# Where the projection of four short chunks falls among the steps, one product's place beside a burst, and three more idle matmuls in the head

## The chip, the core and the metric

The kernel runs on one core of a Trainium2 chip. TensorE (PE in the profile) multiplies matrices, ScalarE (ACT) and VectorE (DVE) work elementwise, GpSimd (POOL) and SyncE (SP) mostly issue DMAs here. The metric is the time of one execution on the device in microseconds (us). Unprofiled, the kernel before takes 773.35 us, the median of three runs (773.33 to 774.28).

## The reference

The input x is 8 sequences of 3008 tokens with 256 channels. Each channel is filtered along the sequence (a real Fourier transform, a product with a complex filter, the transform back), and each of the 24064 tokens then goes through two matrices with a "snake" activation between them:

```python
X = np.fft.rfft(x, axis=1)                       # 8 x 3008 x 256
y = np.fft.irfft(X * (filt_r + 1j * filt_i)[None], n=3008, axis=1)
h = y.reshape(24064, 256) @ w_in                 # 256 -> 2048
s = np.sin(alpha * h)
out = (h + s * s / (alpha + 1e-09)) @ w_out      # 2048 -> 256
```

Inputs and output are float32; the kernel works in float16 with float32 sums.

## The kernel before

**The two halves of the work.** The Fourier filter is a two-stage transform written as matmuls with tables. For a sequence b the parts are: `load_x` (a DMA), `first` or `first_tiled` (matmuls into PSUM tiles `pa`), a turn through DRAM (`load_t2`), `forward` (matmuls into `pb`, a copy to `xf` on ScalarE, and a DMA that swaps the halves of `xf` into `xs`), `product` (VectorE, L257: `xf` times the filter's real part), `cross` (VectorE, L263 and L264: `xs` times the imaginary part, and the sum), `inverse` or `inverse_tiled` (matmuls into `pc`), again a turn through DRAM (`load_t4`), and `last` (matmuls into `pd`, copied into `y`). Sequence 0 is done in the head of the program, before the steady loop, with its own functions.

The second half works on chunks of tokens: 48 chunks, twelve for each pair of sequences, 512 tokens each except the sixth of each pair, which has 384 (chunks 5, 17, 29 and 41; L597). `hidden(k, jb)` (L603) makes one of sixteen tiles of chunk k: two matmuls of 512 (or 384) columns into a PSUM tile `ph`, a sine on ScalarE (`cos_all`, L614), and one operation on VectorE (`v`, L615, called STT below) that also sets the PSUM tile free. `project(k, u)` (L619) is half of a 128-token block of the second product: eight matmuls of 256 columns into `po`. After an odd u of the second block, and of the last block, ScalarE copies the result (L639) and a DMA stores it.

**The order.** All engines execute in the order in which the program is written, and this order comes from the loop at L759. Chunk k has eight steps. A step writes two `hidden` tiles of chunk k, then what is due of the Fourier work (`slot(step)`), then the share of `project` for chunk k-1, then `slot(step + 0.5)`. A chunk of 512 tokens has eight halves to project, one in each step. One of 384 has six for eight steps, so two steps stay without.

The Fourier work lies in the list `pending` with due times in steps, set by formulas at L709 to L742. At certain times, the list `bursts` (L693), four or eight matmul groups come at once: `first_tiled` or `inverse_tiled`. A burst takes two PSUM tiles from the pool `fps` and two from the pool `hps`; each is copied out by ScalarE (two or three of them) and VectorE (two or one). `aside` (L699) moves a `product` or a `cross` that falls shortly before a burst to just behind it.

**PSUM.** The `ph` tiles and the burst's second pair share the four buffers of `hps` in turn: a tile can be begun when the tile four places earlier has been read for the last time, by STT or by the burst's copy. The two buffers of `fps` hold `pa`, `pb`, `pd` and the burst's first pair; the two of `ops` hold `po`.

**The head.** Before the loop, TensorE transforms sequence 0. `spread_alpha` (L349) brings alpha to all partitions with twelve small matmuls into a tile of `hps`. `inverse_table` (L426) turns a table with sixteen transposes into a tile `pse` of `ops`, from which ScalarE makes the table `t_a`. `warm_pe(n)` (L438) issues n matmuls of 512 columns on a zero tile, into a tile of `hps` that nobody reads.

Of the kernel before, what the change touches and what calls it, by code (L numbers as in the profile page):

```python
# [71 lines left out]
def kernel(  # L72
# [276 lines left out]
    def spread_alpha(i):  # L349

        ps = hps.tile([128, 4, 128], FP32, name=f"al_bc_{i}", tag="h")
        for a in range(4):
            for k, part in enumerate(parts):
                nc.tensor.matmul(out=ps[:, a, :], lhsT=one[:, 4 * i + a:4 * i + a + 1].to_broadcast([128, 128]),
                                 rhs=part, start=(k == 0), stop=(k == 2))
        nc.scalar.copy(out=alpha[:, i // 2, 512 * (i % 2):512 * (i % 2) + 512], in_=ps.rearrange("p a b -> p (a b)"))
# [69 lines left out]
    def inverse_table(g):  # L426

        gs = slice(8 * g, 8 * g + 8)
        ps = ops.tile([128, 8, 128], FP16, name=f"pse_{g}", tag="o")
        for i in range(8):  # L430
            for a in range(2):
                nc.tensor.transpose(out=ps[64 * a:64 * a + 64, i, :],
                                    in_=d_t[:, 8 * g + i, 64 - 64 * a:128 - 64 * a], identity=id16)
        nc.scalar.mul(e1_0[:, gs, :], ps, -0.125)
# [3 lines left out]
    def warm_pe(n):  # L438

        warmed.append(n)  # L440
        ps = hps.tile([128, 512], FP32, name=f"warm_{len(warmed)}", tag="h")
        for i in range(n):
            nc.tensor.matmul(out=ps, lhsT=idle[:, 0:128], rhs=idle[:, 0:512], start=True, stop=True)
# [18 lines left out]
    for i in range(16):  # L462
# [7 lines left out]
        if i < 15 and i % 4 == 3:  # L470
            warm_pe((1, 2, 2, 1)[i // 4])
    spread_alpha(0)
    [inverse_table(g) for g in range(2)]
    spread_alpha(1)
    warm_pe((2, 2, 2, 1)[3])
# [127 lines left out]
    def hidden(k, jb):  # L603

        _, c0, n = chunks[k]
        if jb == 0:
            v[k] = vpool.tile([128, 16, 512], FP16, name=f"v_{k}", tag="v")
        ps = hps.tile([128, 512], FP32, name=f"ph_{k}_{jb}", tag="h")
        for cb in range(2):
            nc.tensor.matmul(out=ps[:, 0:n], lhsT=w1[:, cb, jb * 128:jb * 128 + 128],  # L610
                             rhs=y_cols[:, cb, c0:c0 + n], start=(cb == 0), stop=(cb == 1))
            one_between()
        cs = cos_all[:, jb % 4, :]
        nc.scalar.activation(out=cs[:, 0:n], in_=ps[:, 0:n], func=AFT.Sin, bias=float(np.pi / 2))  # L614
        marks["snake"] = nc.vector.scalar_tensor_tensor(  # L615
            out=v[k][:, jb, 0:n], in0=cs[:, 0:n], scalar=-1.0, in1=ps[:, 0:n],
            op0=ALU.add, op1=ALU.subtract)

    def project(k, u):  # L619

        pb, c0, n = chunks[k]
        t, half = divmod(u, 2)
        rest = len(chunks) - 1 - k
        alone = rest == 0 or rest == 1 and t > 1
        if rest == 0 and t > 1:
            t = 5 - t
        if (t % 2 == 0 or alone) and half == 0:
            pso[k] = ops.tile([128, 2, C], FP32, name=f"po_{k}_{t}", tag="o")
        for jb in range(8 * half, 8 * half + 8):
            nc.tensor.matmul(out=pso[k][:, t % 2, :], lhsT=v[k][:, jb, 128 * t:128 * t + 128],  # L630
                             rhs=w2[:, jb, :], start=(jb == 0), stop=(jb == 15))
            if jb % 2:
                one_between()
        last = 128 * (t + 1) == n
        if half == 1 and (t % 2 == 1 or last or alone):
            i0 = t % 2 if alone else 0
            o = opool.tile([128, 2, C], FP32, name=f"o_{k}_{t}", tag="o")
            copy = nc.vector.tensor_copy if rest == 0 else nc.scalar.copy
            copy(out=o[:, i0:t % 2 + 1, :], in_=pso[k][:, i0:t % 2 + 1, :])  # L639
            for i in range(i0, t % 2 + 1):  # L640
                store(o[:, i, :], pb, c0 + 128 * (t - t % 2 + i),
                      (nc.scalar, nc.sync, nc.scalar, nc.scalar) if rest == 0 and t == 3 else
                      (nc.sync, nc.scalar) if rest == 0 or (rest == 1 and t > 2) else
                      (nc.sync,) if rest < 7 else (nc.gpsimd,))
# [39 lines left out]
    def firsts(b):  # L684

        return {2: (37.5, 39.5, 41.5, 43.5), 3: (49.5, 54.5, 60.5, 66.5)}.get(
            b, [48 * b - 105.5 + 8 * ch for ch in range(4)])

    def inverses(b):

        return (63.5, 73.5, 81.5) if b == 2 else [48 * b - 46.5 + 16 * w for w in range(3)]

    bursts = [at for b in range(TILED, B) for at in (*firsts(b), *inverses(b))]  # L693
# [4 lines left out]

    def aside(at):  # L699

        return next((s + 0.05 for s in bursts if s - 1.1 < at <= s), at)

    for at, fn in put_later:
        put(at, fn)
# [6 lines left out]
    for b in range(1, B):  # L711
        s = s1 if b == 1 else Spectral(b)
# [12 lines left out]
        for u in range(12):  # L725
            inv = 24 + 1.21 * u if b == 1 else 57 + 2.2 * u if b == 2 else z - 59 + 4 * u
            fwd = inv - 6
            fwd = clear(fwd)
            put(fwd, s.forward, u, pe=True)
            put(aside(fwd + (0.5 if b == 1 else 1.5)), s.product, u)  # L730
            if s.fused:
                put(aside(fwd + (4 if b == 1 else 4.5)), s.cross, u)
            if b < TILED:
                put(inv, s.inverse, u, pe=True)
# [10 lines left out]
    def slot(at):  # L745

        run = 0
        while pending and pending[0][0] <= at:
            if pending[0][2]:
                if run and pending[0][0] > at - 1:  # L750
                    break
                run += 1
            _, _, _, fn, args = pending.pop(0)
            fn(*args)
# [4 lines left out]
    for k in range(len(chunks) + 1):  # L759
        for j in range(8):  # L760
            if k < len(chunks) and step > 0:
                hidden(k, 2 * j)
                hidden(k, 2 * j + 1)
            slot(step)
            if k > 0:
                n_half = 2 * (chunks[k - 1][2] // 128)
                for u in range(n_half * j // 8, n_half * (j + 1) // 8):
                    project(k - 1, u)
            slot(step + 0.5)
            step += 1  # L770
# [31 lines left out]
```

## Time and profile before

| What | Value |
|---|---|
| Median of three runs | 773.35 us (773.33 to 774.28) |
| The profiled execution: its own time | 774.35 us |
| its span, from first to last instruction | 772.6 us |
| TensorE clock granted | full (1.000) |
| PE busy | 763.0 us, 99% of the span |
| DVE busy | 655.4 us, 85% |
| ACT busy | 610.9 us, 79% |
| POOL busy | 373.1 us, 48% |
| STT (L615), 512 columns | 704 of 682 ns, 449.9 us |
| Sine (L614), 512 columns | 704 of 609 ns, 385.8 us |
| `project` matmuls (L630) | 3008, a group of eight takes 0.87 us |

"Busy" is time with at least one instruction under way. Neighbouring instructions overlap in their rows: a group of eight `project` matmuls is listed as 1.04 us long, yet the next group starts 0.87 us after it. Two STTs in a row start 0.60 us apart, two sines 0.48 to 0.49 us, two burst copies on ScalarE 0.48 us. In what follows durations that add up are such distances from start to start. In a row of the timeline the first number is the start and the second the length; a bracket at the end tells how long the engine was idle before it, and what ended that.

### The profile page before, as it was taken

The numbers are of one execution on the slowest core, as the hardware profiler recorded it, in microseconds if no ns is written. First come the engines' busy times: TensorE is split into PE (matmuls) and PEld (weight loads), VectorE is DVE, ScalarE is ACT, GpSimd is POOL, SyncE is SP. The second block draws the span as 40 slices with busy tenths as digits, with TensorE's granted clock in tenths as the row PEclk, the third lists the DMA queues.
The fourth block names the chain that finished last, engine by engine and source line by source line (L and its number), as shares of the span: only waits on it lengthen the run. The fifth ranks groups of instructions, "written<-read, shape, count | busy, mean of one in ns | idle before, by whom it ended". The sixth has DMA issues, their size and how long they took to land.

```text
span 772.6 us, 17227 instructions
## 1 busy us (share of the span) xinstructions
PE 763.0 (99%) x6038; PEld 517.1 (67%) x6038; DVE 655.4 (85%) x1171; ACT 610.9 (79%) x1205; POOL 373.1 (48%) x652
## 2 busy tenths in 40 slices
PE   8999999999999999999999999999999999999997
PEld 4757766666666667666666676766666766766666
DVE  7887998999988888988889888899888888777774
ACT  6898987898787878877878787888778787777763
POOL 7555455644636456545555646644554645520000
PEclk9999999999999999999999999999999999999999
DMA  9945678854854437544574536754254322511112
GB/s 225 292 108 167 139 172 257 205 131 112 219 145 125 114 92 207 140 114 118 118 197 114 137 94 156 196 144 121 72 145 109 90 69 56 147 35 33 40 36 61
DMA packets 81598, 101.49 MB, mean 131 GB/s; under 512 B 18900, under 2 KB 60880, under 8 KB 81511
## 3 DMA queue, kind: packets, MB, share of 16 engines
q0 software_dynamic: 27520, 47.29, 26.0%
q1 hardware_dynamic: 53426, 52.41, 25.5%
q8 instruction: 47, 0.77, 0.4%
q10 hardware_dynamic: 565, 0.70, 0.3%
q14 instruction: 40, 0.33, 0.1%
HBM read 56.15 MB, written 46.66 MB: 133 GB/s over the span
## 4 chain that ended last, share of the span: by engine, by line
PE 89%; DVE 5%; DMA 2%; ACT 2%; POOL 1%; issue 1%; SPq 0%; POOLq 0%; DVEq 0%
PE po L630 40%; PE ph L610 40%; DVE v L615 3%; PE pd L316 2%; PE pb L243 2%; PE pa L222 2%; DMA xs<-xf 1%; PE pc L293 1%; DMA e_t<-e_tbl 1%; ACT cos_all L614 1%; DVE t_a L479 1%; ACT t_h L185 1%; PE pa L206 0%; PE pd L409 0%; POOL filt_t L365 0%
## 5 line engine op out<-in xcount | busy, mean ns | idle before, releaser
L615 DVE SCALAR_TENSOR_TENSOR v<-cos_all,ph 128x512 f16<-128x512 f32 (+1 forms) x768 | 482.5, 671 | 94.8 <-ACT cos_all L614 90.8
L614 ACT ACTIVATE cos_all<-ph 128x512 f32<-128x512 f32 (+1 forms) x768 | 414.1, 600 | 99.4 <-PE ph L610 98.8
L675 POOL DMA_DIRECT2D out_dram<-o x530 | 291.7, 557 | 246.0 <-ACT o L639 219.5
L610 PE MATMUL ph<-y,w 128*128 128x512 f16 (+1 forms) x1536 | 389.3, 375 | 1.6 <-DVE v L615 1.3
L630 PE MATMUL po<-w,v 128*128 128x256 f16 x3008 | 389.5, 273 | 0.0
L630 PEld LDWEIGHTS <-v 128*128 128x128 f16 x3008 | 290.0, 98 | 84.2 <-issue 0.9
L610 PEld LDWEIGHTS <-w 128*128 128x128 f16 x1536 | 143.3, 98 | 114.1 <-issue 19.3
L639 ACT COPY o<-po 128x512 f32<-128x512 f32 (+1 forms) x95 | 56.0, 590 | 7.7 <-PE po L630 6.8
L185 ACT CAST y<-pd 128x376 f16<-128x376 f32 (+1 forms) x86 | 42.0, 490 | 13.1 <-PE pd L316 8.8
L246 ACT CAST xf<-pb 128x512 f16<-128x512 f32 x84 | 51.0, 608 | 0.9 <-PE pb L243 0.2
L160 POOL DMA_DIRECT2D x<-in_x_dram x48 | 25.6, 538 | 39.0 <-DVE v L615 29.9
L185 ACT CAST t_h<-pa 128x512 f16<-128x512 f32 (+1 forms) x60 | 32.8, 589 | 12.6 <-PE pa L222 11.3
L316 PEld LDWEIGHTS <-t_a 96*128 96x128 f16 x448 | 31.4, 97 | 12.7
L264 DVE TENSOR_TENSOR p<-p,xs 128x512 f16<-128x512 f16 x84 | 35.7, 425 | 2.9
L263 DVE TENSOR_TENSOR xs<-xs,filt_t 128x512 f16<-128x512 f16 x84 | 35.1, 418 | 3.5 <-DMA xs<-xf 3.5
L257 DVE TENSOR_TENSOR p<-xf,filt_t 128x512 f16<-128x512 f16 x84 | 35.0, 418 | 0.0
L185 ACT CAST gt<-pc 128x512 f16<-128x512 f32 x54 | 28.1, 595 | 8.4 <-PE pc L293 8.4
L187 DVE CAST t_h<-pa 128x512 f16<-128x512 f32 (+1 forms) x52 | 33.5, 682 | 0.2
L243 PE MATMUL pb<-t,d_t 128*128 128x256 f16 x168 | 32.1, 273 | 0.0
L316 PE MATMUL pd<-wh_t,t_a 96*128 96x94 f16 x384 | 31.8, 204 | 0.0
L235 POOL DMA_DIRECT2D t<-d x28 | 24.4, 874 | 10.7 <-DMA d<-t_h 10.0
L243 PEld LDWEIGHTS <-d_t 128*128 128x128 f16 x168 | 16.4, 98 | 14.3
(72 smaller groups left out, 276.5 us busy)
## 6 DMA issues: line engine op xcount, KB each, us to landing
t<-d POOLq DMA_DIRECT2D x28, 384.0 KB, 5.0
xs<-xf SPq DMA_DIRECT2D x168, 64.0 KB
t_a<-d SPq DMA_DIRECT2D x28, 384.0 KB
x<-in_x_dram POOLq DMA_DIRECT2D x50, 188.0 KB, 4.4
d<-t_h SPq DMA_DIRECT2D x48, 192.0 KB
d<-gt SPq DMA_DIRECT2D x36, 256.0 KB
out_dram<-o POOLq DMA_DIRECT2D x91, 64.0 KB, 2.1
out_dram<-o POOLq DMA_DIRECT2D x31, 80.0 KB, 3.3
```

The source lines that it names most:

```text
L185: marks["act"] = nc.scalar.copy(out=dst, in_=src)
L243: nc.tensor.matmul(out=ps[:, i, :], lhsT=d_t[:, s, :], rhs=self.t2[s // 6][:, s % 6, :], start=True, stop=True)
L246: nc.scalar.copy(out=self.xf[u], in_=ps)
L263: nc.vector.tensor_tensor(out=xs, in0=xs, in1=f_t[1][:, 2 * u:2 * u + 2, :], op=ALU.mult)
L264: nc.vector.tensor_tensor(out=p, in0=p, in1=xs, op=ALU.add)
L316: nc.tensor.matmul(out=psv[:, i, :], rhs=wi_t if self.b < TILED else wh_t, start=True, stop=True, lhsT=t4_h[ch // 2][0:NK, n0 % 16 + i, cb ...
L610: nc.tensor.matmul(out=ps[:, 0:n], lhsT=w1[:, cb, jb * 128:jb * 128 + 128], rhs=y_cols[:, cb, c0:c0 + n], start=(cb == 0), stop=(cb == 1))
L614: nc.scalar.activation(out=cs[:, 0:n], in_=ps[:, 0:n], func=AFT.Sin, bias=float(np.pi / 2))
L615: marks["snake"] = nc.vector.scalar_tensor_tensor(out=v[k][:, jb, 0:n], in0=cs[:, 0:n], scalar=-1.0, in1=ps[:, 0:n], op0=ALU.add, op1=ALU. ...
L630: nc.tensor.matmul(out=pso[k][:, t % 2, :], lhsT=v[k][:, jb, 128 * t:128 * t + 128], rhs=w2[:, jb, :], start=(jb == 0), stop=(jb == 15))
L639: copy(out=o[:, i0:t % 2 + 1, :], in_=pso[k][:, i0:t % 2 + 1, :])
L675: queues[i % len(queues)].dma_start(out=bass.AP(tensor=out.tensor, offset=out.offset + t0 * C, ap=[*ap, [1, C]]), in_=o_blk[p0:p0 + rows, :])
```

## The change

Three edits. The halves of a 384-token chunk are dealt to the eight steps by rounding the bounds up, not down: before, steps 0 to 7 of the following chunk get 0, 1, 1, 1, 0, 1, 1, 1 halves, after it 1, 1, 1, 0, 1, 1, 1, 0. Chunks of 512 tokens keep one half in each step. This acts at the chunks that follow chunks 5, 17, 29 and 41, which are steps 48 to 55, 144 to 151, 240 to 247 and 336 to 343. The window of `aside` goes from 1.1 to 1.3 steps. Going through all due times, one item changes: `product` 9 of sequence 2, due at 72.3, goes to 73.55, behind the `inverse_tiled` at 73.5. And `warm_pe(3)` stands in the head between `spread_alpha(0)` and the first two calls of `inverse_table`.

```diff
     spread_alpha(0)
+    warm_pe(3)
     [inverse_table(g) for g in range(2)]
     spread_alpha(1)
...
     def aside(at):
-        return next((s + 0.05 for s in bursts if s - 1.1 < at <= s), at)
+        return next((s + 0.05 for s in bursts if s - 1.3 < at <= s), at)
...
             slot(step)
             if k > 0:
                 n_half = 2 * (chunks[k - 1][2] // 128)
-                for u in range(n_half * j // 8, n_half * (j + 1) // 8):
+                for u in range(-(-n_half * j // 8), -(-n_half * (j + 1) // 8)):
                     project(k - 1, u)
             slot(step + 0.5)
```

## The prediction

> **What bounds the kernel now.** I read the page's busy times and chain of waits first, then the waits of each engine, then the timeline where the three edits act.
>
> ```profile
> PE 763.0 (99%) x6038; PEld 517.1 (67%) x6038; DVE 655.4 (85%) x1171; ACT 610.9 (79%) x1205; POOL 373.1 (48%) x652
> PE 89%; DVE 5%; DMA 2%; ACT 2%; POOL 1%; issue 1%; SPq 0%; POOLq 0%; DVEq 0%
> ...
> DVE v L615 <- ACT cos_all L614: 90.8, 179, 1.8
> DVE xs L263 <- DMA xs<-xf: 3.5, 4, 1.9
> PE ph L610 <- DVE v L615: 1.3, 5, 0.6
> ```
>
> TensorE sets the end, and none of its matmuls goes away, so the change can only win or lose PE's waits. The waits count 1.3 us for STT, too little: matmul rows are longer than their distances, so a short wait shows as a longer group. Four `ph` matmuls undisturbed are 1.03 long and the next group follows after 0.87; where PE waits they read 1.19. Around hidden chunk 18 (steps 144 to 147):
>
> ```profile
> 314.34 1.89 PE L610 MATMUL ph<-y,w 128*128 128x512 f16 x8
> 316.04 2.48 DVE L615 SCALAR_TENSOR_TENSOR v<-cos_all,ph 128x512 f16<-128x512 f32 x4 [0.42 <-ACT cos_all L614]
> 317.04 0.75 PE L293 MATMUL pc<-p,e_t 64*64 64x256 f16 x16
> 317.49 1.56 ACT L185 CAST gt<-pc 128x512 f16<-128x512 f32 x3
> 317.98 1.19 PE L610 MATMUL ph<-y,w 128*128 128x512 f16 x4 [0.19 <-DVE v L615]
> 318.92 1.12 ACT L614 ACTIVATE cos_all<-ph 128x512 f32<-128x512 f32 x2
> 319.58 1.28 DVE L615 SCALAR_TENSOR_TENSOR v<-cos_all,ph 128x512 f16<-128x512 f32 x2 [0.46 <-ACT cos_all L614]
> ```
>
> The eight `ph` in one row are step 144's missing half: four tiles within 1.73 us, for which DVE needs 4 x 0.60 = 2.40. The burst then finds its buffers full. It takes 0.94 to the next `ph` (317.04 to 317.98) where an undisturbed one takes 0.56 (158.82 to 159.38), and the next four `ph` 1.02 instead of 0.87: 0.54 us lost. The same 0.54 is lost at chunk 30 (501.68 to 503.65). At chunk 6 the `first_tiled` bursts lose 0.16 each (131.15, 140.72), at chunk 42 there is no burst and no loss. For `aside`:
>
> ```profile
> 178.82 0.42 DVE L257 TENSOR_TENSOR p<-xf,filt_t 128x512 f16<-128x512 f16 x1
> 179.07 0.63 PE L293 MATMUL pc<-p,e_t 64*64 64x256 f16 x16
> 179.15 1.28 DVE L615 SCALAR_TENSOR_TENSOR v<-cos_all,ph 128x512 f16<-128x512 f32 x2
> 179.88 1.19 PE L610 MATMUL ph<-y,w 128*128 128x512 f16 x4 [0.18 <-DVE v L615]
> 181.61 1.28 DVE L615 SCALAR_TENSOR_TENSOR v<-cos_all,ph 128x512 f16<-128x512 f32 x2 [0.58 <-ACT cos_all L614]
> ```
>
> The product stands ahead of the two STTs that PE waits for: 0.25 and 0.17, together 0.42. So 0.54 + 0.54 + 0.32 + 0.42 = 1.82 us is the most that these edits can take from PE's waits.
>
> **Rounding up, chunk 18.** PE after: four `ph` to 315.21, eight `po` (0.87) to 316.08, four `ph` to 316.95, eight `po` to 317.82, a switch of 0.10, the burst from 317.92, the `ph` of tile 4 at 318.48, of tile 5 at 318.92. The second pair of sines now starts when its `ph` is done, and the STTs of tiles 2 and 3 end at 318.03 and 318.63 (0.11 later than before): no wait. Before, tile 5 started at 318.57 with eight `po` fewer, so PE is 318.57 + 0.87 - 318.92 = 0.52 us ahead.
>
> Now DVE. The burst starts 0.88 later (317.92 against 317.04), so do its three copies on ACT, and the sine of tile 4 is written behind them: 318.92 + 0.88 = 319.80. The STT of tile 4 moves from 319.58 to 320.46, and DVE's idle time before it grows from 0.46 to 1.3 us. After this STT, DVE has no idle row until 334.05 (0.11), then 335.96 (0.62): all its work to there runs 0.88 late. What PE has in hand against it, start of a tile less end of the STT four tiles back, is read from the same rows: 0.60 and 0.44 us at tiles 10 and 11, 0.52 and 0.35 at 12 and 13, 0.18 and 0.05 at 14 and 15. PE with its half moved stands, against before, at +0.29 there, so it starts to wait at tile 10, follows DVE, and reaches tile 15 at +0.88. Behind tile 15 comes the second step without a half, so PE passes to chunk 19 about level with before, and waits once more at tile 5, where it had 0.81: +0.13. **Chunk 18 pays all back: +0.13 us.** Bounds: -0.54 (nothing paid back) and +0.88 (DVE's whole delay).
>
> The repayment rests on ACT doing its work in written order. The row bears it out: tile 4's `ph` pair was begun at 317.98 and 318.19, its sine started at 318.92, when the third copy had started at 318.45. The Trainium skill, "Perfetto Trace Analysis", section "Tensor Engine Instruction (MATMUL, LD_WEIGHTS)", says that ACT and DVE are strict FIFOs; the row agrees. Could the sine pass the copies, chunks 18 and 30 would keep their 0.54 each, and the sum would be -1.7.
>
> **Chunk 30** has the same order, but DVE has a gap of 0.10 at 505.95, and PE holds 0.87 and 0.70 at tiles 10 and 11, 0.38 and 0.23 at 14 and 15. The same steps give waits of 0.17 and 0.15 at 14 and 15, tile 15 at +0.61, chunk 31 at 0.88 less than that (the half no longer there): -0.27. It then holds 1.14 to 1.30 us at tiles 4 and 5, enough for DVE's 0.79 and its own 0.27. **-0.27**; bounds -0.54 and +0.88 again.
>
> **Chunk 6.** DVE idles 0.94, 0.90 and 0.50 us (129.21, 136.66, 139.97) within it, so it catches up. PE starts tile 5 at 132.45 against 131.74 with a half more done (0.16 ahead), and tile 12 at 139.05. Two tiles (0.87), the last half (0.87) and the switch bring the second burst to 140.89, tile 14 to 141.45 and tile 15 to 141.88; the STTs they need end at 140.98 and 141.6. Then `last` (0.17), `forward` (0.22), and chunk 7 starts at 142.70 against 143.00: **-0.30**, bounds -0.32 and +0.5 (DVE's delay behind the first burst). **Chunk 42**: DVE idles 0.4 to 0.6 us every other tile, no burst: **0**.
>
> Moved with the halves: at each of the four chunks, two output copies on ACT (0.60 and 0.40 us) and their stores go one step forward. The second now stands ahead of a burst's copies at 6, 18 and 30; it ends about 0.46 after the last `po`, when the burst's first pair is ready (0.10 + 0.45): nothing, and 0.4 on an ACT queue that then delays DVE if that cover goes. POOL issues the stores (0.56 us each) ahead of a `load_x` that they followed; those loads are used eight steps (15 us) later and land in 4.4 us: hidden. SP is passed by only chunk 41's stores, with nothing due. The `xs` copies on SP keep their order.
>
> **The product.** Without it the two STTs start 0.33 us earlier (178.82) and end at 179.50 and 180.10. PE starts tile 4 at 179.63, tile 5 at 180.15 instead of 180.49: **-0.34**. The product goes behind the next pair of STTs and the cross there, which the 0.58 us of idleness before 181.61 doesn't absorb, since those STTs wait for ACT; DVE runs 0.33 late to its next gap (190.43, 0.45), and PE, ahead by 0.34, holds at least 0.98 us in between. Its consumer, the burst at step 81.5, is eight steps off. Bounds: -0.42 and 0.
>
> **The idle matmuls.**
>
> ```profile
> 12.08 0.83 PE L354 MATMUL al_bc<-w,one 128*128 128x128 bf16 x12
> 13.62 1.08 PE L432 MATMUL pse<-w,d_t 128*64 128x128 f16 x32 [0.70 <-DMA d_t<-d_tbl]
> 19.91 0.23 PE L520 MATMUL pc<-p,e_t 128*128 128x128 f16 x1 [0.24 <-DMA e_t<-e_tbl]
> ```
>
> Three at 0.214 us are 0.64, from 12.76 to 13.40, and PE waits for a table's DMA until 13.62: **0**. Were that DMA early, PE would be 0.64 late for ScalarE's tables; they are ready 1.6 us before VectorE's first product (18.84), and the next matmul waits for `e_t` at 19.91. Behind the insertion each `hps` tile takes another buffer, all read out by 12.93. Bounds 0 and +0.64; a gain could come from the clock alone (below).
>
> **Sum**: 0.13 - 0.27 - 0.30 - 0.34 + 0 = -0.78 us. Against the profiled execution's own 774.35 that is 773.57; against the median 773.35, which is 1.00 below it, 772.57, and I say 772.6. What a measurement here can tell from no change is 0.2%, or 1.55 us: under 771.8 or over 774.9.
>
> **Rivals.** *DVE catches up everywhere* (0.22): its delays are hidden, -1.82, 771.5. Chunk 6's idle rows speak for it, chunk 18's fourteen us without one against. *All is paid back* (0.12): the delays of chunks 6 and 30 surface as at 18, and the product's 0.33 meets a wait: about +0.4, 773.8. *A late `xs`* (0.12, the one that ends slower): at 339.11 `cross` made DVE wait 1.87 us for its DMA, and PE lost 0.36 + 0.16 + 0.17 + 0.16 = 0.85 behind it. Chunk 31 with the same order lost nothing, so it hangs on how DMAs fall. The moved stores change that. If the chunks behind all three bursts meet it, 3 x 0.85 - 0.78 = +1.8, 775.1; it is slower than before from the first such wait on (+0.07). That one wait may as well vanish, -0.85 more. *The clock* (0.04): the head's first twelve idle matmuls stand 427 ns apart, later ones 214, so PE starts at half speed. If unprofiled runs dropped back in the idle 0.87 us at 12.7, the five us of PE work to 19.6 would double, some 3 us past `e_t`, and the edit would save that: 770. The trace against it: `al_bc` is 56 ns apart on both sides. The Trainium skill, "TensorE: Matmul & The Clock Gate", section "What's actually happening", asks an idle window of about 3.4 us for the drop; 0.87 is far below, and by that rule nothing is won. *No change at all* is no rival of its own: the order differs.
>
> **How the numbers follow.** The forecast has 0.48, the last 0.02 is unknown. Its own range is 771.9 to 773.5. The range runs from 771.4 (the first rival) to 774.4 (all paid back and part of a late `xs`); left out are the clock and the worst of `xs`, under 0.2. Faster by over 0.2%: most of the first rival, the clock, a little of the forecast, 0.25. Slower: `xs` at its worst, 0.12. Within: 0.63.
>
> **What would show it.** After the change the burst at chunk 18 follows a row of eight `po` and its next `ph` comes after 0.56; the first STT behind it has an idle time near 1.3; `ph` rows of 1.1 to 1.2 appear at tiles 10 to 15. The product at step 74 stands behind the `gt` copy. `ph` at the loop's start stays at 34.84. The forecast is wrong if DVE shows no such idle time, if an `xs` wait over 1 us appears or goes, or if the loop starts elsewhere.

## The result and the profile after

The changed kernel takes 776.16 us (median of 9 runs, 775.38 to 779.97), the kernel before 773.96 us (median of 9). The ratio is 1.0031 with a 95% interval of 1.0017 to 1.0045: **slower by 0.31%, some 2.4 us**. The forecast was 772.6 us and no change that can be measured, with a range to 774.4. It was wrong: the kernel got slower.

The profiled execution after took 776.16 us itself, the one of before 774.35. Their spans differ by 1.8 us (774.4 against 772.6), so these two traces show most of the loss. The page and the waits from 35 us on, after (columns of a wait: total us, number, longest):

```profile
PE 763.2 (99%) x6041; PEld 516.5 (67%) x6041; DVE 654.8 (85%) x1171; ACT 611.5 (79%) x1205; POOL 372.6 (48%) x652
...
DVE xs L263 <- DMA xs<-xf: 5.7, 3, 3.4
PE ph L611 <- DVE v L616: 2.5, 3, 1.8
PE pb L243 <- DVE y L187: 0.2, 1, 0.2
```

PE is still busy 99%, but its waits for an STT have grown from 1.3 to 2.5 us, and the longest from 0.6 to 1.8. The line above it names the cause: `cross` waited 5.7 us on VectorE for `xs` where it had waited 3.5. `xs` is the swapped copy of `xf` that two DMAs of 64 KB on SP's queue make (L250); I call the two the swap.

To see where the time went, I took the start of each hidden chunk's first `ph` in both traces. A chunk's change is the difference between the two traces that it adds:

| stretch | forecast | measured |
|---|---|---|
| head (loop starts at 34.59, was 34.84) | 0 | -0.25 |
| chunk 6, and chunk 7 behind it | -0.30 | +0.03, +0.26 |
| chunk 9 (the product), and chunk 10 | -0.34 | -0.34, +0.08 |
| chunk 18 with the wait that it leaves in chunk 19 | +0.13 | +0.12 |
| chunk 19, the late swap | 0 | +1.56 |
| chunk 30 | -0.27 | -0.43 |
| chunk 31, the late swap | 0 | +0.69 |
| chunk 42 and the others to 46 | 0 | 0 |
| chunk 47 and the end | 0 | +0.09 |
| sum | -0.78 | +1.81 |

The two late swaps are 2.25 us of the 2.59 us between forecast and trace. This is the place in chunk 19 after, in the timeline (columns: start, length, engine, line, operation, tiles, count, and in brackets the idle time before it and what ended it):

```profile
339.31 1.04 PE L631 MATMUL po<-w,v 128*128 128x256 f16 x8
340.57 0.42 DVE L263 TENSOR_TENSOR xs<-xs,filt_t 128x512 f16<-128x512 f16 x1 [3.43 <-DMA xs<-xf]
341.37 1.28 DVE L616 SCALAR_TENSOR_TENSOR v<-cos_all,ph 128x512 f16<-128x512 f32 x2
342.10 1.19 PE L611 MATMUL ph<-y,w 128*128 128x512 f16 x4 [1.75 <-DVE v L616]
```

VectorE takes its work in order, so the STTs of two tiles stand behind `cross` and wait 3.43 us with it. PE has no free `ph` buffer, ends its eight `po` and waits until an STT has run. Before, the same wait was 1.87 us:

```profile
339.11 0.43 DVE L263 TENSOR_TENSOR xs<-xs,filt_t 128x512 f16<-128x512 f16 x1 [1.87 <-DMA xs<-xf]
```

Two things changed ahead of it. The first is on PE. VectorE comes to `cross` at the same time in both (337.24 before, 337.14 after: the start of its row less the idle time). But the `pb` from which the swap follows comes 0.64 us later, because the half of `project` that stood behind it now stands ahead. Before:

```profile
328.06 0.38 PE L243 MATMUL pb<-t,d_t 128*128 128x256 f16 x2
328.27 1.04 PE L630 MATMUL po<-w,v 128*128 128x256 f16 x8
```

and after:

```profile
328.70 0.38 PE L243 MATMUL pb<-t,d_t 128*128 128x256 f16 x2
328.92 0.33 PE L316 MATMUL pd<-wh_t,t_a 96*128 96x94 f16 x4
329.09 1.03 PE L611 MATMUL ph<-y,w 128*128 128x512 f16 x4
```

So the swap is issued 0.64 us later and is wanted at the same time. The second is on the two DMA queues. The timeline of before, POOL and SP:

```profile
328.70 1.09 POOL L160 DMA_DIRECT2D x<-in_x_dram  x2
329.78 0.88 POOL L235 DMA_DIRECT2D t<-d  x1
330.63 2.28 POOL L675 DMA_DIRECT2D out_dram<-o  x4
...
328.83 1.25 SPq L229 DMA_DIRECT2D d<-t_h  x2
330.18 1.82 SPq L250 DMA_DIRECT2D xs<-xf  x2
```

and of after:

```profile
328.82 1.10 POOL L676 DMA_DIRECT2D out_dram<-o  x2
329.92 1.09 POOL L160 DMA_DIRECT2D x<-in_x_dram  x2
331.00 0.89 POOL L235 DMA_DIRECT2D t<-d  x1
...
329.48 1.25 SPq L229 DMA_DIRECT2D d<-t_h  x2
330.82 1.50 SPq L250 DMA_DIRECT2D xs<-xf  x2
```

The output stores of the last block stood behind the loads of `x` and `t`; now they stand ahead. The loads are issued 1.2 us later (331.00 against 329.78 for `t`), SP's swap only 0.64 later. The 384 KB load of `t` is now issued 0.52 us ahead of the second half of the swap (331.51) instead of 1.10. At its old time, 329.78, it would stand 1.73 ahead.

The trace also has sixteen semaphore updates for each of these transfers (the counts by which an engine learns that a DMA has landed), and `cross` starts 0.09 us behind the last. After, fifteen updates of the swap's second half are in by 338.36 and the sixteenth comes at 340.48; those of the load of `t` come by 338.53 and at 340.65. Before, fifteen are in by 337.84 and the sixteenth comes at 339.02. So the wait has two parts. To the fifteenth update the swap's second half took 6.85 us after and 6.96 before, no longer than before; it was issued later against `cross`. On top, one update of sixteen came 2.11 us late, before 1.18.

Chunk 31 has the same pattern without a late update (the sixteenth comes 0.04 us behind): `t` at 517.11, the swap's second half at 517.52, `t` landed at 523.98:

```profile
516.03 1.10 POOL L160 DMA_DIRECT2D x<-in_x_dram  x2
517.11 0.91 POOL L235 DMA_DIRECT2D t<-d  x1
...
516.70 1.52 SPq L250 DMA_DIRECT2D xs<-xf  x2
...
524.15 0.43 DVE L263 TENSOR_TENSOR xs<-xs,filt_t 128x512 f16<-128x512 f16 x1 [1.25 <-DMA xs<-xf]
```

### The profile page after: what moved, and what is told of

Read it like the earlier page. It is cut to its first block, busy times and chain, and to the rows that moved or that the text cites. A ratio compares the mean times of both kernels' runs of the same rounds, so it can differ in the third digit from the quotient of the medians.

```text
span 774.4 us, 17233 instructions
## 1 busy us (share of the span) xinstructions
PE 763.2 (99%) x6041; PEld 516.5 (67%) x6041; DVE 654.8 (85%) x1171; ACT 611.5 (79%) x1205; POOL 372.6 (48%) x652
## 4 chain that ended last, share of the span: by engine, by line
PE 90%; DVE 4%; DMA 3%; ACT 2%; issue 1%; POOL 0%; SPq 0%; ACTq 0%; DVEq 0%
PE po L631 40%; PE ph L611 39%; DVE v L616 3%; PE pb L243 2%; PE pd L316 2%; DMA xs<-xf 2%; PE pa L222 1%; PE pc L293 1%; ACT cos_all L615 1%; PE warm L443 1%; DMA cos_all<-in_x_dram 1%; PE pc L521 1%; PE pb L498 1%; PE pa L465 1%; PE pa L206 0%
```

## The experiments

The theory from the two traces: the halves moved one step forward put their stores ahead of POOL's loads, the loads start later, and the load of `t` falls onto the swap. Its rivals: the loss is made inside the chunks by VectorE's delay behind the bursts; the order on POOL alone does it, whatever the loads meet; the moved half does it by making the swap itself later; or another of the three edits does it. All kernels below compute the whole output.

### The three edits one by one

Round-up alone:

```
range(n_half * j // 8, n_half * (j + 1) // 8)
-> range(-(-n_half * j // 8), -(-n_half * (j + 1) // 8))
```

> The kernel before with the rounding up alone. By the traces of before and after, chunk by chunk, the rounding up should carry the whole loss: +0.03 at chunk 6, +0.26 at chunk 7, +1.68 at chunk 19, -0.43 at chunk 30, +0.69 at chunk 31, together about +2.2 us, ratio 1.003. If the head or the product's place were the cause (rival: the traces' gains there are of one execution), it would be level with before, 1.000.

775.41 us, ratio 1.0028 [1.0014, 1.0042]: nearly the whole loss. Its trace has the late swap too, 1.69 us at chunk 19 and 1.21 at chunk 31, with the sixteenth update only 0.24 and 0.28 us behind the fifteenth:

```profile
327.72 2.22 POOL L675 DMA_DIRECT2D out_dram<-o  x4 [0.72 <-ACT o L639]
329.93 1.09 POOL L160 DMA_DIRECT2D x<-in_x_dram  x2
331.02 0.89 POOL L235 DMA_DIRECT2D t<-d  x1
...
338.84 0.43 DVE L263 TENSOR_TENSOR xs<-xs,filt_t 128x512 f16<-128x512 f16 x1 [1.69 <-DMA xs<-xf]
```

The product alone (`s - 1.1` to `s - 1.3`):

> The kernel before with the wider window of aside alone: one product of sequence 2 behind its burst. The forecast's -0.34 us at chunk 9 should stand (the traces show -0.34 there), and +0.1 at chunk 10: -0.3 us, ratio 0.9997. If DVE pays it back later, 0.

773.75 us, 0.9998 [0.9989, 1.0006]. Its trace has -0.33 at chunk 9 and gives 0.07 back at chunk 10; a gain of 0.26 us is less than this measurement can tell.

The idle matmuls alone (`warm_pe(3)` ahead of `inverse_table`), taken twice:

> The kernel before with the three idle matmuls alone. The loop starts 0.25 us earlier in the trace of after than of before; if the idle matmuls do that, -0.25 us; if it is how the table's DMA falls in an execution, 0 and the loop's start varies by some 0.3 us between executions. If the clock dropped in unprofiled executions, -1 us or more.

774.84 us, 1.0012 [1.0003, 1.0020].

> The three idle matmuls alone, a second time. The first gave +0.9 us (0.2 to 1.5) while its profiled execution, one of its fastest, showed the loop starting level with before. If the idle matmuls cost something in most executions, +0.9 again and a profile that shows where; if the first was the spread of how DMAs fall, within 0.4 us of before.

774.92 us, 1.0009 [1.0000, 1.0018]. Alone they cost 0.7 to 0.9 us by the two medians; the second interval just reaches no cost. The loop starts at 34.84 and 35.45 us in these two, between 34.36 and 35.04 in ten traces without them, and at 34.59 in the trace of the whole change: no common shift. Two more kernels looked for the mechanism: the matmuls in the `fps` buffers instead of `hps`, so that no buffer behind them shifts,

```
warm_pe(n, own=hps, tag="h") ...   warm_pe(3, fps, "f")
```

> The kernel before with the three idle matmuls writing a tile of the pool fps in place of hps. If the cost of +0.8 us in two runs comes from the turn of the hps buffers behind the insertion, it goes: within 0.3 us of before. If it comes from three more matmuls on TensorE in the head, it stays: +0.8 us, 1.001.

774.46 us, 1.0003 [0.9982, 1.0025], and six of them in place of three:

> The kernel before with six idle matmuls at that place in place of three: 1.28 us where TensorE waits 0.7 to 0.9 us for a table, so the tables' transposes start some 0.4 us late. If the loop's start hangs on TensorE there, +1.2 us or more; if the cost comes with the tile and not with the matmuls, +0.8 as with three; if the head has the 1.6 us in hand that the prediction read from the rows, level with before.

774.76 us, 1.0010 [0.9997, 1.0023]. The median shows no doubling, so their own PE time is unlikely to be the cost, though the interval doesn't exclude it. The interval with the other buffers holds both no cost and the cost of e3, so it decides nothing. What they cost alone stays open.

### Moving the loads

The whole change, with the last `load_x` of sequences 5 and 7 half a step and the last `load_t2` of 4 and 6 a whole step earlier:

```
put(... firsts(b)[ch] - 8 - (0.5 if b in (5, 7) and ch == 3 else 0), s.load_x, ch)
put(max(70, z - 77 + 12 * g) - (1 if b in (4, 6) and g == 3 else 0), s.load_t2, g)
```

> The kernel after, with two loads each of chunks 18 and 30 (the last x load of sequences 5 and 7, the last t2 load of sequences 4 and 6) due half a step and one step earlier, so that POOL issues them ahead of the last projected block's stores again, as before the change. Theory 1 (those stores hold the loads back by 1.2 us, the loads then share the DMA engines with the xs swap, and cross waits): the wait of 3.4 us at chunk 19 falls to 1.9 or less, chunk 19 gets back some 1.4 us and chunk 31 some 0.6: total about +0.2 against before, ratio 1.000. Theory 2 (the swap is late because the burst, its copies and its d1 store are later themselves): no difference to after, 1.003.

773.54 us, 0.9993 [0.9972, 1.0014]. `t` is issued at 326.99 and landed at 331.26, before the swap's second half is issued (331.92); `cross` still waits 0.55 us at chunk 19, by a sixteenth update 1.39 us behind the fifteenth, and not at all at 31:

```profile
337.69 0.43 DVE L263 TENSOR_TENSOR xs<-xs,filt_t 128x512 f16<-128x512 f16 x1 [0.55 <-DMA xs<-xf]
```

Then the counter-test on the kernel before: the same loads later (0.9 and 0.5 steps), so that POOL has the order of the changed kernel and nothing else is changed.

> The kernel before with nothing but the order of four loads changed: the last x load of sequences 5 and 7 and the last t2 load of sequences 4 and 6 come half a step to a step later, so that POOL issues them behind the last projected block's stores, as in after. No matmul moves. Theory 1 (the stores ahead of the loads on POOL are enough for the late swap): cross waits 2 to 3.5 us at chunk 19 and over 1 us at chunk 31, and the time rises by 1.0 to 2.0 us, ratio 1.0013 to 1.0026. Rival (it takes the moved projection too, which makes the burst's copies and its d1 store later): level with before, 1.000.

773.86 us, 0.9994 [0.9982, 1.0006], no loss:

```profile
330.25 2.23 POOL L675 DMA_DIRECT2D out_dram<-o  x4 [1.43 <-ACT o L639]
332.47 1.10 POOL L160 DMA_DIRECT2D x<-in_x_dram  x2
333.56 0.89 POOL L235 DMA_DIRECT2D t<-d  x1
...
330.27 1.54 SPq L250 DMA_DIRECT2D xs<-xf  x2
...
337.26 0.42 DVE L263 TENSOR_TENSOR xs<-xs,filt_t 128x512 f16<-128x512 f16 x1
```

The stores stand ahead of the loads as in the changed kernel. But the loads came 3.8 us later than before, not 1.2, and fell behind the swap, and `cross` doesn't wait. So the order on POOL alone is not enough; it matters through when the loads meet the swap. This kernel also keeps the old deal, so its swap is issued 6.3 us ahead of VectorE's turn at `cross`, as before; it doesn't test the later swap.

To hold POOL by about a microsecond, without touching the order, the kernel before was given three copies of a table onto itself ahead of the loads (`for _ in range(3): nc.gpsimd.tensor_copy(out=wi0_t, in_=wi0_t)` at steps 150.45 and 246.45):

> The kernel before with three small copies on POOL (of a table to itself, no longer used) in front of the last x load of sequences 5 and 7, so that this load and the t2 load behind it start about 1 us later while every other order stays. Theory 1b (the loads' start falls together with the d1 store and just in front of the xs swap; a delay of 1.2 us does harm, one of 3.8 us as in the run with the loads last doesn't): cross waits over 1.5 us at chunk 19 and about 1 at chunk 31, time +0.7 to +2 us, ratio 1.001 to 1.0026. Rival (it takes the moved projection): level, 1.000.

773.95 us, 1.0005 [0.9996, 1.0014]. It missed its aim: `t` was issued at 333.37, just behind the swap's second half (333.22), not ahead of it, and there was no wait. That is not because the swap was fast: its second half took 5.6 us to the fifteenth update at chunk 19 and 6.3 at chunk 31, and the old deal left it 6.3 and 6.5.

The deciding kernel is the whole change with only the last `load_t2` of sequences 4 and 6 moved, to 4.9 steps later:

```
put(max(70, z - 77 + 12 * g) + (4.9 if b in (4, 6) and g == 3 else 0), s.load_t2, g)
```

> The kernel after with one thing changed: the last t2 load of sequences 4 and 6 comes 4.9 steps later, so that POOL issues it some 9 us later, behind the xs swap in front of which it stood by 0.4 to 0.5 us. The projection, the stores and the x loads stay as in after. If the swap is late because this load is issued just ahead of it, the waits at chunks 19 and 31 go and the time falls by about 2 us against after, to 0.9990 to 1.0010 of before. Rival (the moved projection or the stores in front of the x load do it, through the x load and the d1 store): still 1.0025 to 1.0035.

**773.27 us, 0.9994 [0.9986, 1.0002]: the loss is gone**, with everything else of the change in place. But the profiled execution of this kernel, which took 774.6 us and so 1.3 us more than its median, still has a late swap at chunk 19:

```profile
330.22 1.09 POOL L160 DMA_DIRECT2D x<-in_x_dram  x2
337.92 3.35 POOL L676 DMA_DIRECT2D out_dram<-o  x6 [6.60 <-ACT o L640]
341.26 0.90 POOL L235 DMA_DIRECT2D t<-d  x1
...
331.12 1.66 SPq L250 DMA_DIRECT2D xs<-xf  x2
...
339.71 0.42 DVE L263 TENSOR_TENSOR xs<-xs,filt_t 128x512 f16<-128x512 f16 x1 [2.28 <-DMA xs<-xf]
```

Here no load of `t` is near; the two loads of `x` (188 KB each), issued 0.90 and 0.35 us ahead of the swap's first half, landed at 336.46 and 337.78. Fifteen updates of the swap's second half were in by 337.46, almost in time for VectorE (337.43). The sixteenth came at 339.61, and it alone made the wait. So the swap is fast enough once the load of `t` is away, and the late sixteenth update is a second cause, which this edit doesn't remove.

### Another deal, and the best of the parts

Halves dealt 1,1,1,0,1,0,1,1, so that the first and the last steps keep theirs and the stores at the chunk's end stay where they were:

```
for u in ([j] if n_half == 8 else [(0, 1, 2, None, 3, None, 4, 5)[j]] if j not in (3, 5) else []):
```

> The kernel before with the halves of the short chunks dealt 1, 1, 1, 0, 1, 0, 1, 1 to the eight steps: the burst at the second step has its projection in front of it as in after, and the last two halves stay in the last two steps as before, so the last block's stores stay behind the loads. Theory 1: no late swap beyond that of before, the 0.54 us in front of the bursts of chunks 18 and 30 go, and chunk 18 pays back what DVE is late (up to 0.6): -0.3 to -0.8 us, ratio 0.999 to 0.9996. Rival (any moved projection makes the swap late): +1 to +2 us.

775.86 us, 1.0027 [1.0018, 1.0036]. By the step of the `pb` it has as many halves done as the old deal, so the swap keeps its time ahead of `cross` (6.2 and 6.3 us). No swap is late, yet it is as slow: it loses 0.45 us at chunk 6, 1.12 at chunk 18 and 0.68 at chunk 30, inside the chunks. The step without a half now stands just where VectorE is behind, and PE waits there:

```profile
323.54 1.17 PE L610 MATMUL ph<-y,w 128*128 128x512 f16 x4
324.54 0.33 PE L316 MATMUL pd<-wh_t,t_a 96*128 96x94 f16 x4
325.50 1.19 PE L610 MATMUL ph<-y,w 128*128 128x512 f16 x4 [0.63 <-DVE v L615]
```

So the rival that the loss is made inside the chunks describes a real mechanism, but that of another deal.

The change without the idle matmuls, with loads earlier (`load_x` 0.6, `load_t2` 1 step):

> The kernel after without the three idle matmuls, and with the last x load and the last t2 load of chunks 18 and 30 due 0.6 and 1 step earlier, in front of the last block's stores, the x load ahead of the t2 load as in before (in the run with the loads first the t2 load had come ahead of the x load as well). Theory 1: the gain of that run does not hang on the order of the two loads, and without the idle matmuls it is the best so far: -0.5 to -1.3 us, ratio 0.9983 to 0.9994. If it was the t2 load's place ahead of the x load that helped, +1 us or more.

773.53 us, 0.9993 [0.9985, 1.0002]. `t` is issued 1.84 us ahead of the swap's second half, and no `cross` waits at 19 or 31:

```profile
328.83 1.09 POOL L160 DMA_DIRECT2D x<-in_x_dram  x2 [1.52 <-DVE v L615]
329.92 0.88 POOL L235 DMA_DIRECT2D t<-d  x1
...
331.15 7.08 SPq L250 DMA_DIRECT2D xs<-xf  x4
...
337.37 0.42 DVE L263 TENSOR_TENSOR xs<-xs,filt_t 128x512 f16<-128x512 f16 x1
```

Last, what had gained in the traces alone: the product, the rounding up at chunk 30 only (`up = 7 if k == 30 else 0`), and the loads earlier as in e7.

> The kernel before with the product behind its burst, the rounding up at chunk 29 alone (worked off in chunk 30, where the traces kept 0.43 us), and the last x load and t2 load at chunks 18 and 30 in front of the last block's stores. Sum by the traces: -0.34 + 0.08 - 0.43 = -0.7 us, and what the swap's waits cost before in most executions (0 to 0.9): -0.7 to -1.4 us, ratio 0.9982 to 0.9991.

772.98 us, 1.0003 [0.9985, 1.0022]; the same kernel in another set of runs:

> The best version again, for its interval, which a few slow executions had widened: -0.7 us, 0.9985 to 0.9995.

773.26 us, 0.9988 [0.9969, 1.0007]. With the load of `t` 4.9 steps later instead of earlier:

> The best version so far (the product behind its burst, rounding up for chunk 29 alone) with those two t2 loads 4.9 steps later in place of a step earlier. If the swap behind chunk 18 is then never late, 0.6 to 0.9 us less than the best version in the executions where it was late: -1 to -1.7 us against before, 0.9978 to 0.9987. If the load meets another swap there, no gain on the best version.

773.10 us, 0.9990 [0.9969, 1.0012]. Their medians lie 0.7 to 0.9 us below that of before, and every interval holds 1. No version can be said to beat the kernel before.

### The lead and the wait

All traces together, with the lead of `t` (its issue to the issue of the swap's second half) and the wait of `cross`:

| lead of the load of `t` | chunk 19: wait, us | chunk 31: wait, us |
|---|---|---|
| 0.41 to 0.52 us | 3.43 (after), 1.69 (e1) | 1.25 (after), 1.21 (e1) |
| 0.84 to 1.13 us | 1.87 (before), 0.70 (e2), 0.63 (e3), 0.75 (e8), 1.48 (g2), 0.45 (g3), 0.68 (g4), 0.72 (h3) | 0 to 0.27 (before, e2, e3, e8, g2, g3) |
| 1.8 us and more | 0 (e6, e7), 0.55 (e4, lead 4.9) | 0 to 0.05 (e4, e6, e7, g4, h3) |
| behind the swap | 0 (e5, g1, h2), 2.28 (h1, by one late update) | 0 (e5, g1, h2), 0.12 (h1) |

A shorter lead goes with a longer wait, but the rows of one lead spread: at chunk 19, 1.1 us gave 0.45 to 1.87. The lead doesn't explain it. The wait is what the swap takes less the time that it has, so here are both, from the issue of its second half, the first to the fifteenth update:

| load of `t` | the swap took, chunk 19, us | chunk 31, us |
|---|---|---|
| 0.41 to 0.52 us ahead | 6.85 (after), 7.03 (e1) | 6.56 (after), 6.27 (e1) |
| 0.84 to 1.13 us ahead | 6.55 to 6.96 | 6.40 to 6.60 |
| 1.8 us and more ahead | 4.29 to 5.25 | 4.28 to 5.37 |
| behind | 2.85 (e5), 4.96 (h2), 5.57 (g1), 5.62 (h1) | 2.53 (e5), 3.77 (h2), 6.29 (g1), 5.22 (h1) |

| deal | time to VectorE's turn, chunk 19, us | chunk 31, us |
|---|---|---|
| old, or last halves kept (e6) | 6.24 to 6.37 | 6.27 to 6.60 |
| rounded up | 5.22 to 5.67 | 5.12 to 5.56 |

Between 0.41 and 1.13 us the lead makes no difference. The old deal had just time enough for a swap beside the load of `t`: waits of up to 0.75 us at chunk 19 cost PE nothing there. In the changed kernel the time is 0.7 us shorter at chunk 19 and 1.2 at chunk 31, and isn't enough unless the load is moved. No run has the short lead with the old deal, so this is read from the times of the traces and not tested by a kernel of its own.

The rest of the spread is the sixteenth update. At chunk 19 it came 0.96 to 2.16 us behind the fifteenth in five of seventeen traces (after, h1, e4, before, g2) and at most 0.37 in the others; at chunk 31 at most 0.64 in all. In those five a packet of 16 KB on the queue that the profile calls "instruction" had run for about 1 us and ended 1.0 to 1.9 us before the late update; at chunk 31 there is none. But such a packet ran near chunk 19's swap in all seventeen, so it is a suspect and no more.

The trace of before is one of the five: nine traces with the old deal at chunk 19 have that chunk 0.84 us shorter. With these 0.84 taken out, e1's trace, which has no late update, is 1.3 us longer than it from the loop's start on. It is the fastest of e1's twelve executions, whose median is some 2.2 us up. How much of the rest is late updates no run shows.

## Why the prediction was wrong

**The step that failed** is the paragraph on what is moved with the halves, which put the DMAs at nothing by asking for their order and their users alone. "The `xs` copies on SP keep their order" is true and leaves out when they run. A half that stood between the swap's `pb` and its `cross` now stands ahead of both: the time from the issue of the swap's second half to VectorE's turn fell from 6.36 to 5.62 us at chunk 19 and from 6.58 to 5.37 at chunk 31, while the swap took 6.85 and 6.56 us, as before. The sentence ahead of it, "those loads are used eight steps (15 us) later and land in 4.4 us: hidden", holds for their users. But I didn't ask what else is in flight when they run, and named only `load_x`. The load that stands right behind it on POOL, 384 KB of `t`, was held back with the swap and stayed just ahead of it. Where it was moved away the swap took 5.25 us (e7) and 5.62 (h1) at chunk 19, and the loss was gone.

**The rival of a late `xs`** had the direction and the place, and 0.12 of the chance. It said that the moved stores change how DMAs fall, which is half of the mechanism. Its price, three times 0.85, was close in sum (2.55 against 2.25) by luck, put together otherwise: chunk 19 lost 1.56 on top of what it had lost, 0.93 of it by the later sixteenth update; chunk 31 lost 0.69, chunk 7 nothing by this. I took the one large wait of before (1.87 us) as chance and gave it an even sign, "that one wait may as well vanish". Of the 1.87 us, 1.18 were the late sixteenth update and did vanish in most other traces. The other 0.69 were no chance: the swap had less time than it took, and my own rows had a sign for it. I had the burst 0.88 us later and chunk 19 "about level with before", so the swap behind the burst had to come closer to a `cross` in chunk 19. The sign that I named, "an `xs` wait over 1 us appears", did come, at chunk 31.

**Point by point.**
- *Chunk 18* was right in mechanism and size: +0.12 for +0.13. The burst follows eight `po`, the next `ph` comes 0.57 after it, and VectorE then idles 1.15 us (1.3 forecast) where it had idled 0.46:

```profile
316.72 1.04 PE L631 MATMUL po<-w,v 128*128 128x256 f16 x8
317.68 0.63 PE L293 MATMUL pc<-p,e_t 64*64 64x256 f16 x16
318.25 1.04 PE L611 MATMUL ph<-y,w 128*128 128x512 f16 x4
...
320.23 1.28 DVE L616 SCALAR_TENSOR_TENSOR v<-cos_all,ph 128x512 f16<-128x512 f32 x2 [1.15 <-ACT cos_all L615]
```

  The `ph` rows of tiles 10 to 15 read 1.16, 1.11 and 1.19, as said. This is the repayment that rests on ACT keeping its order, as the Trainium skill ("Perfetto Trace Analysis", section "Tensor Engine Instruction (MATMUL, LD_WEIGHTS)") has it; 1.15 us of idleness agrees.
- *Chunk 30* was right in direction and mis-sized: -0.43 for -0.27. If the whole 0.54 was gained, VectorE's delay took 0.11 of it instead of 0.27.
- *Chunk 6* was wrong by 0.59 with what it leaves behind. I followed VectorE's STTs against `ph` only. With the half gone from between them, two `pd` tiles and a `pb` come in a row, and PE waits for the copy that frees an `fps` buffer, 0.34 us in all:

```profile
134.45 0.54 DVE L187 CAST y<-pd 128x376 f16<-128x376 f32 x1
134.54 0.33 PE L316 MATMUL pd<-wi_t,t_a 96*128 96x94 f16 x4
135.05 0.38 PE L243 MATMUL pb<-t,d_t 128*128 128x256 f16 x2 [0.18 <-DVE y L187]
```

  The chunk ends level, and 0.26 more is lost in chunk 7, at the burst at 152.1, where VectorE still is late. That VectorE "catches up" was wrong for chunk 6.
- *The product*: -0.34 as forecast, exactly where it was said, and 0.08 of it lost in chunk 10, which I had down as covered. The first `ph` behind it comes at 179.66 (179.88 before), and the next pair of STTs finds a longer idle time, 0.92 for 0.58:

```profile
179.10 0.63 PE L293 MATMUL pc<-p,e_t 64*64 64x256 f16 x16
179.66 1.11 PE L611 MATMUL ph<-y,w 128*128 128x512 f16 x4
...
181.65 1.28 DVE L616 SCALAR_TENSOR_TENSOR v<-cos_all,ph 128x512 f16<-128x512 f32 x2 [0.92 <-ACT cos_all L615]
```

- *The idle matmuls* were put at 0 and bounded at +0.64. In the whole change's trace the loop even starts 0.25 earlier, within what it varies without them. Alone they cost 0.7 to 0.9 us (e3, e8), a little above that bound, and h1, which has them, shows no such cost. The granted clock is full in all these traces (0.999 or 1.000), and neither e3 nor e8 is faster, so the rival of the clock fell.

Without the two late swaps, the head and the end, the terms that I worked out came to -0.28 us where -0.78 was forecast. The sign was right and 0.5 were missing: chunk 6 with what it leaves in chunk 7 was 0.59 worse, chunk 30 0.16 better. h1 measures 0.9994, about -0.5 us, with an interval that holds both and no change. A term that was left at zero, 2.25 us, was three times as large as the whole forecast.

## What to carry to other kernels

When a step is moved, list what each of its DMAs is moved past, and then look not only at order and at the users of the DMAs that come later. For every short transfer that is waited for soon, take the time from its issue to its consumer's turn, before and after the edit, and compare it with what the transfer takes beside the loads in flight. Here 0.7 to 1.2 us were taken from a transfer that had none to spare. A wait in the profile that already falls on such a transfer (1.87 us here) is a sign that it has none, even where part of the wait is chance. A long load that isn't needed soon can be put behind the short transfer; moving one load by 4.9 steps took back the whole 2.4 us.

## What was unexpected of the hardware

The swap is 2 x 64 KB, and its second half took 6.3 to 7.0 us to the fifteenth update with the load of 384 KB issued 0.41 to 1.13 us ahead, 4.3 to 5.4 with 1.8 us and more, and 2.5 and 2.9 in e5, where the loads of `x` came behind too. It doesn't stand alone on its queue: two stores of 192 KB (`d<-t_h` in the rows above) are issued just ahead of it. In the trace's DMA packets after, the first packet of the swap (1 KB) starts at 335.13, 4.3 us after its issue; until then its queue moved packets of the stores (2 KB), from 330.74 on. In e5 the swap's first packet starts 1.5 us after its issue. In all four cases with a lead of 0.41 to 0.52 us, the fifteenth updates of swap and load lie within 0.2 us of each other. The Trainium skill, "DMA: Bandwidth & Descriptors", section "Queues, rings and completion order", says that each DMA engine takes turns between the queues that have work, a whole packet at a time. The times fit that: a short copy behind 384 KB of its own queue lasts about as long as the loads on the other. No row tells on which engine a packet ran, so the turns themselves are not shown.

One update of sixteen can come 1 to 2 us behind the other fifteen, and a consumer waits for it: 2.11 of the 3.43 us after, 2.16 of 2.28 in h1. I did not find what makes it late. What three idle matmuls cost when put alone into a stretch where PE waits for a table anyway was not settled either.
